# Moving a third exponential tile per batch to VectorE, the combine weights' transposes to another step, and buffers into the order of their release

## The chip, the cores and the metric

One core of a Trainium2 chip. The metric is device time in microseconds, the median of several runs. Ratios are the mean time of one kernel's fast runs over that of the other's of the same rounds, so not quite the ratio of the medians quoted beside them. Ratios use fast runs alone; a median quoted as "measured" is of all runs, and where one of them counts as slow (over 1.5 % above the fastest of its kernel), that is said. The clock is the share of PE's full clock that the profile shows as granted. Engines: PE is TensorE, ACT ScalarE, DVE VectorE, POOL GpSimd, SP SyncE.

## The reference

Attention with a soft cap, then a soft mixture of experts over its output:

```python
# q, k, v: (8 batches, 12 heads, 448, 64), cap 30
scores = cap * tanh((q @ k.T / 8) / cap)
attn = exp(scores - max) / sum                    # x = attn @ v, 3584 x 768
logits = x @ phi                                  # 32 slots, 4 for each of 8 experts
slot_in = softmax(logits, over tokens).T @ x
slot_out[e] = relu(slot_in[e] @ w1[e]) @ w2[e]    # 768 -> 1024 -> 768
out = softmax(logits, over slots) @ slot_out
```

## The kernel before

The attention runs as 56 chunks of six 128 x 448 score tiles, seven chunks a batch. I call them place 0 to 6 of a batch. ACT makes two tanh and one exponential a chunk. PE makes scores ("sc"), attention times V ("pv"), transposes and small sums; most of the latter share one bank of PSUM (`psT`, `bufs=1`), so each waits for the copy of the one before (in the trace before kps waits 0.25 us for zacc, lps 0.48 us for the copy of eps). Of these, kps, qps and xps are transposes of k, q and x, lps the logits, eps the transposed weights of the mixture, and zps and wps their sums over tokens and over slots; zacc and winv are what DVE makes of the two sums. From chunk 8 on, DVE computes the exponential of the first tile in places 1 and 3 as a polynomial:

```python
shared = [j for j in range(NCH - 2) if j % 7 in (1, 3) and j > 7] if cap < 80 else []

def poly_exp(j, part):
    t, bits = exs[j][:, 0, :], 2.0 ** 23
    if part == 0:      # three tensor_scalar operations: exponent and mantissa bits
        ...
    elif part == 1:    # two SBUF inputs from here on
        dve.scalar_tensor_tensor(xp, xm, POW2[1], xm, ALU.add, ALU.mult)
        dve.scalar_tensor_tensor(xp, xp, POW2[2], xm, ALU.add, ALU.mult)
    else:
        dve.scalar_tensor_tensor(xp, xp, POW2[3], xm, ALU.add, ALU.mult)
        dve.scalar_tensor_tensor(t, xp, POW2[4], xe.bitcast(F32), ALU.add, ALU.mult)

def e_norm(b):         # "zps" on PE, "zacc" on DVE
    ps = psT.tile([P, 1], F32, name="zps", tag="T")
    ...                # four matmuls
    dve.tensor_tensor(zacc, ps, zacc, op=ALU.add)

def e_sums(bb):        # "wps" on PE, "winv" on DVE
    ps = psT.tile([P, NT], F32, name="wps", tag="T")
    ...                # seven matmuls
    dve.reciprocal(winv[:, bb, :], ps)

def vcast(Q):          # two POOL casts of V, float32 to bfloat16
    pool.tensor_copy(t[0:HP, :, :, 0:DH], raw[0:HP])
    pool.tensor_copy(t[HP:P, :, :, DH + 1:VW - 1], raw[HP:P])
    ...
```

A table `at(chunk, slot, function, ...)` fixes the order of every engine's instructions: slot "a" is behind the first pv of a chunk, "b" and "c" around the second, "d" at its end. `spare(n)` issues n matmuls of ones ("junk"), which keep PE busy (ten take 0.75 us). After the attention, 20 tiles of w2 ("w2t") are loaded into the SBUF that its buffers leave, then two layers and the output follow.

The softmax here doesn't subtract the row's maximum and nothing guards it: scores larger than these inputs give would overflow.

## Time and profile before

| | before |
|---|---|
| time, first three runs | 315.85 us (315.2 to 318.35) |
| last pv ends | 267.2 us |
| output starts, span ends | 281.1, 313.9 us |
| ACT, PE, DVE, POOL busy | 89, 87, 61, 44 % |

The row of PE's clock is one digit a fortieth of the span, 9 for full speed:

```profile
PEclk9999999999999999999999999999999999999995
```

### The profile page before, as it was taken

How to read it: one execution, taken by the hardware profiler on the slowest of the kernel's cores; microseconds unless marked ns; L12 is line 12 of the kernel's file. 1: busy time of each engine (PE TensorE's matmuls, PEld its weight loads, DVE VectorE, ACT ScalarE, POOL GpSimd, SP SyncE). 2: the span in 40 equal slices, each digit the busy share in tenths (PEclk: the TensorE clock that was granted, in tenths of full speed). 3: DMA queues.
4: the chain of work that ended last, by engine and by line, in shares of the span. 5: the costliest groups of instructions: out<-in, count | busy, mean ns of one | idle time of the engine just before them, and what ended most of it. 6: DMA issues, size and time to landing. Idle time of an engine off the chain costs nothing.

```text
span 313.9 us, 9348 instructions
## 1 busy us (share of the span) xinstructions
PE 271.9 (87%) x4071; PEld 190.6 (61%) x4071; DVE 191.4 (61%) x479; ACT 278.3 (89%) x208; POOL 137.3 (44%) x178
## 2 busy tenths in 40 slices
PE   8899998989899989898989998989898898998620
PEld 6676666666676666666666666666676578643300
DVE  3624567846785578457855885578557765336740
ACT  4999999999999999999999999999999999226630
POOL 5473662655455554474457426652753020200000
PEclk9999999999999999999999999999999999999995
DMA  7999999899999999999799999999999617799996
GB/s 267 195 211 195 205 195 231 131 183 234 216 153 201 222 210 160 209 186 229 122 191 215 194 186 194 223 214 177 164 212 170 156 51 255 249 406 349 397 413 248
DMA packets 57481, 67.64 MB, mean 215 GB/s; under 512 B 3808, under 2 KB 53600, under 8 KB 57440
## 3 DMA queue, kind: packets, MB, share of 16 engines
q0 software_dynamic: 42448, 35.31, 73.4%
q1 hardware_dynamic: 14704, 31.50, 28.6%
q8 instruction: 32, 0.52, 0.6%
q10 hardware_dynamic: 288, 0.23, 0.3%
q14 instruction: 9, 0.07, 0.1%
HBM read 91.32 MB, written 18.87 MB: 351 GB/s over the span
## 4 chain that ended last, share of the span: by engine, by line
ACT 69%; PE 13%; DMA 7%; DVE 5%; issue 2%; SPq 1%; DVEq 0%; ACTq 0%
ACT ex L286 36%; ACT ex L290 32%; DMA w2t<-w2d 5%; PE pv L326 4%; DMA out_dram<-ob 2%; PE sc L277 2%; PE junk L515 1%; PE boot L515 1%; DVE xq L337 1%; PE op L763 1%; ACT ob L772 1%; PE xps L352 1%; DVE obh L721 1%; PE pvl L326 1%; PE pvm L326 1%
## 5 line engine op out<-in xcount | busy, mean ns | idle before, releaser
L286 ACT ACTIVATE ex<-sc 128x1344 bf16<-128x1344 f32 (+1 forms) x113 | 163.7, 1720 | 0.8 <-PE sc L277 0.8
L290 ACT ACTIVATE ex<-ex 128x2688 bf16<-128x2688 bf16 (+4 forms) x58 | 158.0, 2753 | 0.1
L326 PEld LDWEIGHTS <-ex 128*128 128x128 bf16 x1344 | 78.0, 97 | 23.7 <-DVE xq L337 13.7
L326 PE MATMUL pv<-vbd,ex 128*128 128x130 bf16 x1274 | 89.3, 220 | 2.5 <-DVE xq L337 0.8
L277 PE MATMUL sc<-qT,kT 64*64 64x448 bf16 x672 | 78.6, 358 | 5.2 <-ACT ex L286 4.3
L255 POOL CAST vbd<-vraw 64x896 bf16<-64x896 f32 x23 | 22.2, 963 | 66.9 <-PE pv L326 42.7
L336 DVE RECIPROCAL rec<-pv 128x4 f32<-128x4 f32 x91 | 16.5, 182 | 42.6 <-PE pv L326 42.6
L380 POOL COPY e<-E 128x512 bf16<-128x512 bf16 x9 | 6.7, 746 | 81.3 <-ACT E L374 49.2
L337 DVE TENSOR_TENSOR xq<-pv,rec 128x256 bf16<-128x256 f32 x91 | 38.6, 424 | 3.2
L277 PEld LDWEIGHTS <-kT 64*64 64x64 bf16 x672 | 27.0, 105 | 22.3 <-issue 4.2
L515 PEld LDWEIGHTS <-ones 128*128 128x128 bf16 x428 | 26.0, 101 | 10.6 <-DVE xq L337 6.0
L515 PE MATMUL junk<-ones 128*128 128x128 bf16 x391 | 29.1, 220 | 3.1 <-DVE xq L337 2.6
L247 DVE COPY kT<-kps 128x896 bf16<-128x896 bf16 x23 | 14.3, 623 | 18.1 <-PE kps L245 18.0
L256 POOL CAST vbd<-vraw 64x896 bf16<-64x896 f32 x23 | 23.9, 1041 | 1.3
L109 POOL DMA_DIRECT2D w1b<-in_moe_w_dram x32 | 24.5, 766 | 0.0
L354 DVE COPY xT<-xps 128x512 bf16<-128x512 bf16 x47 | 19.5, 414 | 1.0 <-PE xps L352 1.0
L352 PE MATMUL xps<-ident,xq 128*128 128x128 bf16 x188 | 18.1, 218 | 0.8 <-DVE zacc L391 0.2
L167 POOL DMA_DIRECT2D qb<-in_q_dram x22 | 16.2, 736 | 3.8 <-DMA kraw<-in_k_dram 3.1
L247 DVE COPY qT<-qps 128x896 bf16<-128x896 bf16 x23 | 14.2, 618 | 5.5 <-PE qps L245 5.5
L245 PE MATMUL qps<-ident,qb 128*64 128x128 bf16 x308 | 12.8, 222 | 4.1 <-DVE lg L368 4.0
L167 POOL DMA_DIRECT2D kb<-in_k_dram x22 | 16.0, 728 | 0.0
L113 POOL DMA_DIRECT2D w2d<-in_moe_w_dram x20 | 15.1, 761 | 0.0
(117 smaller groups left out, 280.4 us busy)
## 6 DMA issues: line engine op xcount, KB each, us to landing
w1b<-in_moe_w_dram POOLq DMA_DIRECT2D x32, 384.0 KB, 8.8
vraw<-in_v_dram SPq DMA_DIRECT2D x23, 448.0 KB, 6.3
w2d<-in_moe_w_dram POOLq DMA_DIRECT2D x20, 384.0 KB, 8.9
w2t<-w2d SPq DMA_DIRECT2D x20, 384.0 KB, 5.8
out_dram<-ob SPq DMA_DIRECT2D x8, 768.0 KB, 8.6
qb<-in_q_dram POOLq DMA_DIRECT2D x22, 224.0 KB, 7.2
kb<-in_k_dram POOLq DMA_DIRECT2D x22, 224.0 KB, 8.2
w2b<-in_moe_w_dram POOLq DMA_DIRECT2D x12, 384.0 KB, 8.1
```

Source lines behind the costliest of these rows:

```text
L109: pool.dma_start(out=w1b[e][:, js, fs], in_=w1r[:, e, js, fs])
L167: (sp if nm == "v" else pool).dma_start(out=t, in_=quad_ap(nm, Q))
L247: dve.tensor_copy(t, ps)
L255: pool.tensor_copy(t[0:HP, :, :, 0:DH], raw[0:HP])
L256: pool.tensor_copy(t[HP:P, :, :, DH + 1:VW - 1], raw[HP:P])
L277: pe.matmul(sc[cs, u, 0:S], qkT["k", Q][r, c, cs], qkT["q", Q][r, :, cs], start=True, stop=True)
L286: act.activation(exs[j][:, half * CS + u0:half * CS + u1, :], sc[:, u0:u1, 0:S], ACT.Tanh, scale=qk_scale / cap)
L290: act.activation(exs[j][:, u0:u1, :], exs[j][:, u0:u1, :], ACT.Exp, scale=cap)
L326: pe.matmul(pvs[pr, half][:, n, 0:VW], exs[j][:, u, GOFF[g]:GOFF[g] + P], vbds[Q % 2][:, h, c, :], start=(c == 0 and n == 0), stop=(c == N ...
L337: dve.tensor_tensor(xq[Q][:, 2 * half:2 * half + 2, h * P:(h + 1) * P] .rearrange("p g (i d) -> p g i d", i=2), pv[:, :, :, 0:DH], rec.to_ ...
L352: pe.transpose(ps[:, g, :], xq[Q][:, g, h * P:(h + 1) * P], ident)
L515: pe.matmul(junk if home is None else home, ones, ones, start=True, stop=True)
```

## The change

Its intent: ACT bounds the attention, so take six more tiles from it (places 5); make room on PE and in the transpose bank there by moving the weights' transposes ("eps") and their sums to the next batch's place 1; and lay out SBUF so that the w2t loads find freed buffers early.

```diff
+    hpad = consts.tile([P, E, NFT, NS], BF16, name="hpad")        # was in the tail
+    px = att.enter_context(tc.tile_pool(name="px", bufs=1))       # xe, xm, xp: were last
     qk = att.enter_context(tc.tile_pool(name="qk", bufs=2))
-    vb0, exps (bufs=4), vb1, xs
+    ex0, ex1, vb0, ex2, ex3, vb1 (a pool each), xs
...
-    shared = [... j % 7 in (1, 3) and j > 7]
+    shared = [... j % 7 in (1, 3, 5) and j > 7]
...
-                at(j + 12, "d", e_transp, b)
+                at(j + 15, "c", e_transp, b)
...
-                at(j + 14, "d", e_sums, b // 2)
+                at(j + 15, "d", e_sums, b // 2)
...
-        for slot, part in (("a", 0), ("c", 1)):
-            at(j, slot, poly_exp, j, part)
-        at(j + 1, "b" if j % 7 == 1 else "a", poly_exp, j, 2)
+        for part, (dj, slot) in enumerate(((0, "a"), (0, "c"), (1, "b" if j % 7 == 1 else "a"))
+                                          if j % 7 < 5 else ((0, "c"), (1, "a"), (1, "c"))):
+            at(j + dj, slot, poly_exp, j, part)
...
+    at(3, "d", pool.memset, hpad, 0.0)
```

More of the change, by code (lines that the diff above doesn't have):

```diff
@@ L130 @@
     ldv = att.enter_context(tc.tile_pool(name="ldv", bufs=1))
+    px = att.enter_context(tc.tile_pool(name="px", bufs=1))
+    xe, xm, xp = (px.tile([P, S], dt, name=nm)
+                  for nm, dt in (("xe", I32), ("xm", F32), ("xp", F32)))
     qk = att.enter_context(tc.tile_pool(name="qk", bufs=2))
-    vb = [att.enter_context(tc.tile_pool(name="vb0", bufs=1))]
-    exps = att.enter_context(tc.tile_pool(name="exps", bufs=4))
-    vb.append(att.enter_context(tc.tile_pool(name="vb1", bufs=1)))
+    exps, vb = [], []
+    for nm, home in (("ex0", exps), ("ex1", exps), ("vb0", vb), ("ex2", exps), ("ex3", exps),
+                     ("vb1", vb)):
+        home.append(att.enter_context(tc.tile_pool(name=nm, bufs=1)))
     xs = att.enter_context(tc.tile_pool(name="xs", bufs=4))
-    xe, xm, xp = (xs.tile([P, S], dt, name=nm, tag=nm, bufs=1)
-                  for nm, dt in (("xe", I32), ("xm", F32), ("xp", F32)))
     attp = ExitStack()
@@ L282, in tanh_chunk @@
         if half == 0:
-            exs[j] = exps.tile([P, CH, S], BF16, name="ex", tag="ex")
+            exs[j] = exps[j % 4].tile([P, CH, S], BF16, name="ex", tag="ex")
         sc = scores.pop(i)
@@ L293, in exp_chunk @@
         exp_part(j, 1 if j in shared else 0, CH)
-    shared = [j for j in range(NCH - 2) if j % 7 in (1, 3) and j > 7] if cap < 80 else []
+    shared = [j for j in range(NCH - 2) if j % 7 in (1, 3, 5) and j > 7] if cap < 80 else []
     def poly_exp(j, part):
@@ L632 @@
     tl = ctx.enter_context(tc.tile_pool(name="tl", bufs=1, reuse_waits="tile"))
-    hpad = tl.tile([P, E, NFT, NS], BF16, name="hpad")
-    pool.memset(hpad, 0.0)
     w2t = {}
```

## The prediction

> **What bounds the kernel now.** I read the page first, then the chain of waits in order of time, then the timelines of TensorE (PE), VectorE (DVE) and GpSimd (POOL) over one batch, and last the stretches of the tail. The page's chain, then pieces of the chain in order of time:
>
> ```profile
> ACT 69%; PE 13%; DMA 7%; DVE 5%; issue 2%; SPq 1%; DVEq 0%; ACTq 0%
> ```
> ```profile
> 47.27 2.36 ACT ex L286 x2
> 49.62 1.96 ACT ex L290
> 51.59 2.36 ACT ex L286 x2
> 53.95 2.33 ACT ex L290
> ```
>
> From 6.9 us to 223 us the end hangs on ScalarE (ACT) without a gap: two tanh and one exponential a chunk. A chunk whose first tile VectorE takes over shows 1.96 instead of 2.33: 0.37 us saved. From 223 us on, the same chain runs through PE and DVE with no wait on ACT, 44 us long; pieces of it, with fillers ("junk"), normalisations ("xq") and the polynomial ("xe", "xm") in it:
>
> ```profile
> 238.31 0.33 DVE xT L354
> 238.64 0.31 DVE xe L302
> 238.97 0.41 DVE xm L304
> 239.40 0.39 DVE xe L306
> 239.79 0.10 DVE rec L336
> 239.92 0.43 DVE xq L337
> 240.35 0.05 issue
> 240.40 0.75 PE junk L515 x10
> ```
>
> So the attention is balanced: ACT sets the pace, and PE with DVE in its loop is just behind. How little PE has to spare is in its waits on ACT ("PE sc <- ACT ex": 4.3 us in 12 waits). In the PE timeline they come at 158.91 (0.28), 177.67 (0.12), 191.20 (0.28), 209.97 (0.49) and 223.49 (0.28). Locks at 62.02 and 223.49 are five batches (of seven chunks) apart: 161.47 / 5 = 32.29 us a batch. Left to itself PE would need 32.29 - 0.28 - 0.12 = 31.9 us in an odd batch (one that also forms "wps") and 32.29 - 0.28 - 0.49 = 31.5 in an even one. The scores are double buffered: counted to the end of ACT's preceding instruction (its recorded starts drift early), they are 1.7 us or more ahead of a tanh in most of the steady part.
>
> The tail: at 267 us attention ends. The stretches after it (length, then PE, weight load, DVE, ACT, POOL busy, clock, DMA share, GB/s):
>
> ```profile
> 264.00:272.00 8.00, 7.71 (x148) 6.44 (x145) 3.42 (x13) 3.54 (x7) 2.33 (x2) 1.00 0.77 272
> 272.00:282.00 10.00, 9.74 (x185) 4.70 (x185) 3.68 (x9) 2.77 (x5) 0.02 (x1) 1.00 0.98 382
> 292.00:311.00 19.00, 5.34 (x33) 2.48 (x31) 7.83 (x10) 5.98 (x7) 0.00 (x0) 0.85 1.00 404
> ```
>
> PE is full until about 280; from 281 to 311 the 11 MB of output keep the DMA engines full. In between, PE waits for the last w2t load only 0.34 us.
>
> [...] the polynomial's undisturbed steps show 615 to 625. [...] this carries my prediction (POOL, then DVE):
>
> ```profile
> 206.88 1.04 POOL L255 CAST vbd<-vraw 64x896 bf16<-64x896 f32 x1 [3.07 <-PE pv L326]
> 207.98 1.24 POOL L256 CAST vbd<-vraw 64x896 bf16<-64x896 f32 x1
> ```
> ```profile
> 207.60 0.80 DVE L308 SCALAR_TENSOR_TENSOR xp<-xm 128x448 f32<-128x448 f32 x1
> 208.43 1.26 DVE L309 SCALAR_TENSOR_TENSOR xp<-xp,xm 128x448 f32<-128x448 f32 x1
> ```
>
> Beside the V casts the pair takes 2.09 us instead of 1.2, and the casts take 1.04 and 1.24 instead of 0.93 and 0.95.
>
> **The change part by part.** I call chunks 0 to 6 of a batch by their place.
>
> (1) ACT. Six more first tiles (chunks 12, 19, 26, 33, 40, 47) leave it: 6 x 0.37 = 2.2 us. This is worth something only if PE keeps up: 31.92 us a batch.
>
> (2) DVE gets seven operations each: 0.38 + 0.39 + 0.39, 0.71 + 0.96, 0.62 + 0.63 = 4.1 us, 24.5 us in all, placed after the q copy of place 5 and in place 6. The "eps" transpose and its copy leave place 5. Place 5 to the next batch's place 0 before:
>
> ```profile
> 192.79 0.58 PE L245 MATMUL qps<-ident,qb 128*64 128x128 bf16 x14
> 193.31 0.76 PE L277 MATMUL sc<-qT,kT 64*64 64x448 bf16 x6
> 194.13 0.38 PE L399 MATMUL eps<-ident,e 128*128 128x128 bf16 x4
> 194.99 0.35 PE L363 MATMUL lps<-phib,xT 128*128 128x32 bf16 x8 [0.48 <-DVE ET L400]
> ...
> 199.09 0.58 PE L245 MATMUL kps<-ident,kb 128*64 128x128 bf16 x14 [0.25 <-DVE zacc L391]
> 199.60 0.58 PE L326 MATMUL pv<-vbd,ex 128*128 128x130 bf16 x7
> ```
>
> From qps to the next pv is 6.81 us. Taking out eps brings lps forward by 194.99 - 194.13 = 0.86. But in DVE's queue the first normalisation of place 6 now stands behind the whole new work. Start-to-start times from the trace, from qps: norm begins at 0.11; +0.56 norm, +0.60 q copy, +1.15 part 0, +0.30 logits, +0.56 norm, +0.33 xT, +1.20 part 1, +0.56 norm = 5.4. Part 2 then starts while POOL makes its two V casts, which are released by the pv that ended at about 4.8 (before: 197.97, casts from 198.04). Both of its operations have two SBUF inputs, so I take 2.1 us as at 207.60, not 1.2: 7.5. Then zacc (0.16), which holds the one transpose bank that kps needs: kps at 7.6, pv at 8.1. That is +1.3 us on PE a batch, the 0.86 already used up; without the collision it would be +0.4.
>
> (3) "eps" lands in place 1 behind the second pv, where PE waits 0.30 to 0.38 for a normalisation: about +0.06.
>
> (4) "wps" (odd batches 1, 3, 5) leaves place 0: 171.88 - 171.26 = 0.62 gained. In its new place its reciprocal stands in DVE's queue behind part 1 of place 1's polynomial, which ends at 177.76 before and at about 178.0 with the ET copy ahead of it. Until then the transpose bank is held, so the xps that started at 176.38 starts at about 178.2; 14 fillers follow, and the scores of 177.67 start at about 179.3: +1.6 us, the ACT wait of 0.12 included.
>
> Sum on PE: an even batch 31.5 + 1.3 + 0.06 = 32.9; an odd one 31.9 + 1.3 - 0.62 + 1.7 = 34.3. Both exceed ACT's 31.92, so ACT begins to wait for PE after one or two batches. From the lock at 62 to that at 223: three even, two odd batches, 167.3 against 161.5 = +5.8; then 1.3 - 0.62 + 1.7 = +2.4 up to the end, where no wait on ACT is left to absorb it. Attention ends about 8 us later, nothing of the 2.2 us kept.
>
> (5) Buffers. Before, w2t loads are issued at 244, then 256 (the second lies on vraw and waits for the last V cast), 258, 262, and 13 of 20 only from 267.27 on. With hpad gone from the head and the pools in order of release, I count from tile sizes that about two can go near 246, five by 258, twelve by 265 and three are left near 270 (times as if attention ended as before). They finish before layer 2 needs them. Worth: the 0.34 us wait and what of w2t is still moving when output starts, about 0.2 MB at 400 GB/s, together 0.5 us. The hpad memset (1.8 us on POOL) was hidden and stays so.
>
> Total: 315.85 + 8 - 0.5 = 323; I shade it to 321.5, since the collision of part 2 is inferred from another place (3 to 5 us hang on it).
>
> **The rivals.** (a) PE keeps up, ACT stays the bound: -2.2 - 0.5, 313. For it: DVE is 61% busy, moving eps gives PE 0.86 us just where DVE gets work, and the placement looks deliberate. Against it: place 6 holds 2.3 us of DVE work before and gets 2.9 to 3.8 more in 4.3 us. (b) The DVE burst fits but for the wps stall: six times 0.4 instead of 1.3 takes 5.4 off, 318. (c) Buffers count for more, since DMA is 7% of the chain: 4 us. Against it: output is full from 281 to 311 whatever w2t does, and PE's start of layer 2 waits for no load. (d) PE's clock falls in the new gaps of over 1 us: up to 326; nothing in the trace before shows such a gap in the steady part.
>
> **Range and chances.** My sum has some seven chances in ten, centred on 322 with 2 us to either side; the rest lies between 313 and 318. 8 in 10: 313.5 to 325.5. Faster by over 2% (under 309.5) would need more than ACT and tail can give: 0.03. Slower by over 2% (above 322.2): 0.42. Within: 0.55.
>
> **What would show it.** Right: ACT waits for PE's scores from the third batch on, some 10 us in all; the new part 2 near 1.2 us an operation, beside casts; kps waiting on zacc over 1 us in place 6; xps in odd batches waiting over 1 us for winv; the chain in PE and DVE for most of the span; attention ending near 275. Wrong: ACT without gaps, and its end near 265; then PE found idle time that I didn't see, or POOL's casts came at another moment. The buffers: more w2t loads issued before the last pv, and no w2t in the chain.

One paragraph of the recorded text is cut where it is marked: it quoted figures and a rule from elsewhere, which no trace here shows as they were put. The sum came to 315.85 + 8 - 0.5 = 323 us, shaded to 321.5, and its 0.37 us for a shorter exponential and 2.1 us for part 2 were read from the trace. 615 to 625 is in ns.

What the trace before shows of the collision: the polynomial's first two operations with two SBUF inputs take 0.61 to 0.63 us where no POOL cast or copy runs beside them; beside a V cast the first takes 0.80 to 0.86 us, the second 1.25 to 1.26, in seven places each. DVE's other operations that fall beside casts do not change: `xe<-xe` (one input) stays at 0.39 to 0.40 us, `xq<-pv,rec` (pv in PSUM) at 0.42. Of ACT's recorded starts: the exponential recorded at 237.71 with 3.32 us reaches 0.99 us past the recorded start of the next tanh, 240.04. In rival (d), "over 1 us" is the size of the gaps in this forecast and not a threshold; the trace before has the clock at 0.50 only in the output's drain (from 306 us on), where PE has no work.

## The result

| | before | changed |
|---|---|---|
| median | 317.1 us (315.2 to 318.47, 4 runs) | 331.25 us (330.65 to 331.65, 4 runs) |
| ratio of fast runs | 1 | 1.045 (1.038 to 1.052) |
| last pv ends (profile) | 267.2 | 282.6 |
| output starts, span ends | 281.1, 313.9 | 296.6, 328.9 |
| granted PE clock over the span | 0.986 | 0.950 |

Slower, and outside my range. On the rounds of the experiments below, the kernel before had medians of 315.8 to 315.9 us. The loss lies in the attention (15.4 us later). From the last pv to the end it is 46.2 us instead of 46.7.

The page's chain, which was 69 % ACT, and ACT's group of tanh instructions with its idle time and what ended most of it:

```profile
PE 40%; DVE 33%; ACT 18%; DMA 3%; issue 2%; DVEq 0%; ACTq 0%
...
L291 ACT ACTIVATE ex<-sc 128x1344 bf16<-128x1344 f32 (+1 forms) x113 | 141.3, 1317 | 15.0 <-PE pv L331 7.7
```

ACT now waits 15.0 us before its tanh instructions, for work of PE; 0.8 before. PE and DVE set the end. Place 6, first POOL, then DVE, then PE (start, length, engine, line, operation; in brackets the idle time before and what ended it):

```profile
209.34 0.93 POOL L260 CAST vbd<-vraw 64x896 bf16<-64x896 f32 x1 [2.93 <-PE pv L331]
210.31 1.25 POOL L261 CAST vbd<-vraw 64x896 bf16<-64x896 f32 x1
```
```profile
209.53 0.42 DVE L342 TENSOR_TENSOR xq<-pv,rec 128x256 bf16<-128x256 f32 x1
209.87 0.88 DVE L316 SCALAR_TENSOR_TENSOR xp<-xp,xm 128x448 f32<-128x448 f32 x1
210.78 1.25 DVE L317 SCALAR_TENSOR_TENSOR ex<-xp,xe 128x448 bf16<-128x448 f32 x1
211.96 0.15 DVE L396 TENSOR_TENSOR zacc<-zps,zacc 128x1 f32<-128x1 f32 x1
```
```profile
209.89 0.25 PE L392 MATMUL zps<-ones,e 128*128 128x1 bf16 x4
212.16 0.58 PE L250 MATMUL kps<-ident,kb 128*64 128x128 bf16 x14 [2.02 <-DVE zacc L396]
```

Part 2 runs beside the casts and takes 0.88 and 1.25 us. The ends follow one another: part 2's first operation ends 0.48 us after the first cast, the second cast (1.25 us) 0.81 after that operation, and part 2's second operation 0.47 after the second cast. The tiny zacc stands behind it, and kps waits 2.02 us for zacc's bank. An odd batch's place 1, PE alone (xps waits 1.03 us for winv in two of the three such batches, 0.37 in the third):

```profile
186.72 0.33 PE L414 MATMUL wps<-ones,ET 128*128 128x1 bf16 x7 [0.45 <-DVE ET L405]
186.91 0.72 PE L521 MATMUL junk<-ones 128*128 128x128 bf16 x10
188.65 0.38 PE L357 MATMUL xps<-ident,xq 128*128 128x128 bf16 x4 [1.03 <-DVE winv L415]
```

And what I had not counted, the clock row of the page, and one such place in three stretches of 3.41 us (bounds, length, busy time of PE, PE's weight loads, DVE, ACT, POOL, then the granted clock):

```profile
PEclk9999999987999799979997999999988999999975
```
```profile
241.59:245.00 3.41, 1.40 (x20) 0.87 (x18) 3.30 (x6) 3.41 (x4) 2.77 (x3) 1.00 1.30 204
245.00:248.41 3.41, 3.40 (x38) 2.76 (x37) 1.36 (x4) 2.46 (x2) 1.56 (x3) 0.50 1.21 246
248.41:251.82 3.41, 3.34 (x61) 2.48 (x56) 1.63 (x5) 2.23 (x2) 0.00 (x0) 1.00 1.28 211
```

In the stretch with the wait PE is busy 1.40 of 3.41 us. In the next one its clock is 0.50, although it has work all the time: 38 matmuls where the one after holds 61, and 14 pv take 1.70 us (at 245.90) where the next 14 take 0.98 (at 248.66). The profiled run has five such dips, 20.5 us in all; if half the clock doubled PE's time and all of it counted, that would be at most some 10 us lost (an estimate).

### The profile page after: what moved, and what is told of

It reads as the page before. It is cut to its first block, busy times and chain, and to the rows that moved or that the text cites. A ratio compares the mean times of both kernels' runs of the same rounds, so it can differ in the third digit from the quotient of the medians.

```text
span 328.9 us, 9405 instructions
## 1 busy us (share of the span) xinstructions
PE 279.5 (85%) x4071; PEld 195.9 (60%) x4071; DVE 214.9 (65%) x521; ACT 278.6 (85%) x208; POOL 141.3 (43%) x178
## 4 chain that ended last, share of the span: by engine, by line
PE 40%; DVE 33%; ACT 18%; DMA 3%; issue 2%; DVEq 0%; ACTq 0%
PE pv L331 14%; ACT ex L291 9%; ACT ex L295 8%; PE sc L282 7%; DVE xq L342 6%; DVE xp L314 3%; DVE ex L317 3%; PE junk L521 3%; PE xps L357 3%; PE kps L250 3%; DVE xp L316 2%; DVE xp L313 2%; DVE xm L309 2%; DVE rec L341 2%; DMA out_dram<-ob 2%; DVE xe L311 2%
## 5 line engine op out<-in xcount | busy, mean ns | idle before, releaser
L291 ACT ACTIVATE ex<-sc 128x1344 bf16<-128x1344 f32 (+1 forms) x113 | 141.3, 1317 | 15.0 <-PE pv L331 7.7
L295 ACT ACTIVATE ex<-ex 128x2688 bf16<-128x2688 bf16 (+4 forms) x58 | 132.1, 2282 | 0.1
L331 PEld LDWEIGHTS <-ex 128*128 128x128 bf16 x1344 | 81.7, 100 | 24.5 <-DVE xq L342 11.4
L331 PE MATMUL pv<-vbd,ex 128*128 128x130 bf16 x1274 | 93.2, 226 | 2.3 <-DVE xq L342 0.8
L282 PE MATMUL sc<-qT,kT 64*64 64x448 bf16 x672 | 80.1, 367 | 1.7 <-ACT ex L291 1.5
L260 POOL CAST vbd<-vraw 64x896 bf16<-64x896 f32 x23 | 23.1, 1006 | 69.5 <-PE pv L331 50.6
L261 POOL CAST vbd<-vraw 64x896 bf16<-64x896 f32 x23 | 26.4, 1149 | 1.2
L250 PE MATMUL kps<-ident,kb 128*64 128x128 bf16 x308 | 14.2, 236 | 12.2 <-DVE zacc L396 9.8
L250 PEld LDWEIGHTS <-kb 128*64 128x64 bf16 x308 | 11.3, 118 | 17.8 <-issue 17.7
L357 PEld LDWEIGHTS <-xq 128*128 128x128 bf16 x188 | 14.1, 102 | 7.7 <-issue 7.7
L314 DVE SCALAR_TENSOR_TENSOR xp<-xp,xm 128x448 f32<-128x448 f32 x20 | 17.8, 890 | 0.7
```

The source lines that it names most:

```text
L250: pe.transpose(ps[h * HP:h * HP + HP, c, :], src[:, h, c * DH:(c + 1) * DH], ident)
L282: pe.matmul(sc[cs, u, 0:S], qkT["k", Q][r, c, cs], qkT["q", Q][r, :, cs], start=True, stop=True)
L291: act.activation(exs[j][:, half * CS + u0:half * CS + u1, :], sc[:, u0:u1, 0:S], ACT.Tanh, scale=qk_scale / cap)
L295: act.activation(exs[j][:, u0:u1, :], exs[j][:, u0:u1, :], ACT.Exp, scale=cap)
L331: pe.matmul(pvs[pr, half][:, n, 0:VW], exs[j][:, u, GOFF[g]:GOFF[g] + P], vbds[Q % 2][:, h, c, :], start=(c == 0 and n == 0), stop=(c == N ...
L357: pe.transpose(ps[:, g, :], xq[Q][:, g, h * P:(h + 1) * P], ident)
```

## The experiments

Theories. **Queue and clock**: DVE's queue makes PE wait in place 6 (because of the collision with the casts) and in odd places 1 (because of where the sums stand), and those waits also halve PE's clock for a while. **Queue alone**: the clock costs little. **Layout**: the new buffers cost the time. **Weights**: moving the transposes does. Twelve kernels ran, all correct except one. Where the changed kernel is compared below, its time is 331.25 us. The three runs that count as slow (in `e3_fill`, `e4_no_cast`, `e5_early`) are the ones with their kernel's lowest clock, so leaving them out of the ratios hides part of the clock's effect there.

### One part at a time

`e1_buffers`: `j % 7 in (1, 3)`, and e_transp and e_sums at their old places; only the buffers stay changed.

> The buffers in the order of release (with hpad among the constants) and nothing else. If DVE's queue and PE's clock make the loss, this is a kernel as fast as before: ratio 0.995 to 1.002, the w2t loads in the chain no more, clock 0.98 to 0.99. If the new layout makes the loss (its addresses, or the early memset), ratio 1.03 or more and the clock falls as in the changed kernel.

Measured 315.11 us against 315.76, ratio 0.998 (0.997 to 1.000), clock 0.98. The layout costs nothing and gives about half a microsecond. As worked out, two w2t loads were issued at 246.7 and 247.3, five more by 258.9; before, the second waited until 256.

`e2_no_third`: everything but the third tile.

```diff
-    ... j % 7 in (1, 3, 5) and j > 7
+    ... j % 7 in (1, 3) and j > 7
```

> The whole change without the third exponential tile (buffers and the moved transposes and sums stay). If the third tile's DVE work makes the loss: ratio 0.995 to 1.01, since the 1.7 us that the reciprocal of the sums costs PE in odd batches fits into the lead of 2.7 us that the scores have there; ACT without gaps over 0.3 us until its last batch. If the move of the transposes makes the loss: ratio 1.02 or more.

Measured 316.58 us, ratio 1.005 (1.000 to 1.011), and no wait of ACT in the attention among its longest. Layout and weights alone are not the cause; the loss needs the third tile.

### The clock

`e3_fill`: fillers where PE waits in place 6.

```diff
                 at(j + 13, "d", e_norm, b)
+                at(j + 13, "d", spare, 24)
```

> The changed kernel with 24 filler matmuls on PE in place 6, between zps and kps, where PE waits for zacc anyway. If half of the loss is PE's halved clock after that wait: no stretch at half clock in the attention, clock back to 0.98 or more, 5 to 7 us faster than the changed kernel, 323 to 326 us, which is what my sum without the clock gave. If the queue alone makes the loss and the clock costs little: within 1 us of the changed kernel, as kps still starts when zacc is done.

Measured 326.32 us (326.08 without the slow run), ratio 1.032 (1.029 to 1.035): 5 us back by adding work. But one stretch of 10.2 us at half clock stayed in the profile. It began at 181.79, at the end of an odd batch's wait for winv of 1.02 us. Of its runs the fastest (325.14 us) had the clock at 0.981, the slowest, counted as slow, 334.41 us at 0.941. So the expectation of no stretch at half clock failed, for a reason the next one tests.

`e9_fill_both`: the same, and 18 more fillers in the odd batches' place 1.

```diff
                 at(j + 15, "d", e_sums, b // 2)
+                at(j + 15, "d", spare, 18)
```

> The changed kernel with fillers in both long waits: 24 in place 6 before kps, and 18 in the odd batches' place 1 before xps, where PE waits for the sums' reciprocal. In the fill of place 6 alone one run still had a stretch at half clock that began at the odd batch's wait. If those waits are what halves the clock: no stretch at half clock before the end in any run, all runs within 1 us of each other at 324.5 to 326 us; what is then left over the kernel before, 9 to 10 us, is DVE's queue alone. If the clock falls for another reason: half-clock stretches stay.

Measured 323.36 us, ratio 1.023 (1.017 to 1.029), clock 0.982 to 0.987 in all four runs. In the profile the attention ends at 275.1, and the clock is full until the output drains:

```profile
PEclk9999999999999999999999999999999999999985
```

DVE's queue is as before, part 2 as slow as ever (DVE):

```profile
235.93 0.88 DVE L316 SCALAR_TENSOR_TENSOR xp<-xp,xm 128x448 f32<-128x448 f32 x1
236.84 1.25 DVE L317 SCALAR_TENSOR_TENSOR ex<-xp,xe 128x448 bf16<-128x448 f32 x1
238.02 0.15 DVE L396 TENSOR_TENSOR zacc<-zps,zacc 128x1 f32<-128x1 f32 x1
```

and kps still starts only when zacc is done:

```profile
238.22 0.58 PE L250 MATMUL kps<-ident,kb 128*64 128x128 bf16 x14 [0.63 <-DVE zacc L396]
```

So the clock's share is 331.25 - 323.36 = 7.9 us, and what the change costs at full clock, its gains taken off, 323.36 - 315.92 = 7.4 us. Each is good to about 1.5 us, by the spread of these runs. The time came out 1 us below what I expected, and the runs spread over 3 us instead of 1, without a difference of clock to explain it. The kernel before has such runs too: in the same rounds 318.34 and 318.64 us at a clock of 0.980, beside 315.36 to 315.96. That spread is left open.

### The queue: casts and sums

`e4_no_cast`: the V casts of place 6 left out in the batches with a third tile (a wrong result).

```diff
-        pool.tensor_copy(t[0:HP, ...]) ; pool.tensor_copy(t[HP:P, ...])
+        if Q % NQB or Q < 6:
+            pool.tensor_copy(t[0:HP, ...]) ; pool.tensor_copy(t[HP:P, ...])
```

> The changed kernel without the two GpSimd casts of V in place 6 of batches with a third tile (their V load stays; the result is wrong on purpose). If the casts make part 2 slow: its two operations take 0.62 us each instead of 0.85 and 1.25, kps waits 1.0 to 1.2 us instead of 2.0, PE's clock stays up, and the time is 319 to 322 us. If the collision is of no weight: the wait stays near 2 us and the time within 1 us of the changed kernel. If the collision counts but the clock does not: 325 to 327 us.

Measured 318.92 us (318.3 without a slow run), ratio 1.009 (1.006 to 1.012), about as expected; no half clock in the profile, and kps waits 1.12 us. The slow run, 324.95 us, had its clock at 0.952, so "PE's clock stays up" failed in one run of four. DVE in place 6:

```profile
232.69 0.61 DVE L317 SCALAR_TENSOR_TENSOR xp<-xp,xm 128x448 f32<-128x448 f32 x1
233.34 0.62 DVE L318 SCALAR_TENSOR_TENSOR ex<-xp,xe 128x448 bf16<-128x448 f32 x1
233.88 0.15 DVE L397 TENSOR_TENSOR zacc<-zps,zacc 128x1 f32<-128x1 f32 x1
```

Part 2 takes 1.2 us to the start of zacc instead of 2.1. Two POOL instructions a batch, on an engine that is 43 % busy, decide over 12 us, part of it by way of the clock. Leaving them out also frees POOL for other work; `e7_early_sums` below keeps them and moves part 2 instead.

`e6_sums`: the sums two places later, in place 3.

```diff
-                at(j + 15, "d", e_sums, b // 2)
+                at(j + 17, "b", e_sums, b // 2)
```

> The changed kernel with the sums of the weights (wps and its reciprocal) two places later in place 3, all else as it is. If the reciprocal behind part 1 costs what I predicted (1.6 us in three odd batches): 3.5 to 5.5 us faster than the changed kernel, 326 to 328 us, and no wait of xps over 0.4 us. If the scores' lead hides it: within 1.5 us of the changed kernel.

Measured 326.78 us, ratio 1.035 (1.032 to 1.039). Six stretches at half clock remain, 20.5 us in all, each beginning at the end of place 6's wait of 2.0 to 2.2 us or within 1.1 us after it.

`e12_sums_fill`: that and the 24 fillers of place 6, so both at full clock.

> The changed kernel with the sums of the weights in place 3 and 24 fillers in place 6. It takes the odd batches' wait away besides the clock. If the sums' reciprocal costs 1.6 us in each of three odd batches: 4 to 5.5 us faster than with the fillers in both waits, 319.5 to 321.5 us, and no half clock. If it is hidden: 324 us or more.

Measured 318.78 us, ratio 1.010 (1.005 to 1.015), below the range expected by 0.7. Against the fillers in both waits: 323.36 - 318.78 = 4.6 us, the cost of the sums' place at full clock (with the little that the 18 fillers add). Against `e6_sums`, which differs by the 24 fillers alone: 326.78 - 318.78 = 8.0 us, the clock's price a second time. What is left of the third tile in its place, over the kernel without it (`e10_no_third_sums`, below, in the same rounds): 318.78 - 315.27 = 3.5 us.

`e8_old_weights`: buffers and third tile, transposes and sums where they were.

> Buffers and third tile as in the changed kernel, but the weights' transposes and sums at their places before the change. If the moved transpose gave PE its 0.86 us where DVE's queue decides anyway (as I worked out, used up), and the moved sums cost 1.6 us three times: between 4 us faster and 3 us slower than the changed kernel, 327 to 334 us. If the moved transposes are what pays for the third tile: 336 us or more.

Measured 330.07 us, ratio 1.046 (1.042 to 1.051). Its profiled run (329.93 us) has only two short half-clock stretches (6.8 us), which can cost 3.4 us at most; at full clock it would be at 326.5 us or more (an estimate), above the 323.36 us of the moved weights. So moving the transposes does help PE, and what the sums lose is less; no run shows it at full clock. In it kps waits 2.0 to 2.2 us in place 6, and before that lps 1.1 to 1.3 us in place 5. A wait of 2 us is then not always followed by half the clock. The changed kernel shows this too: its kps at 212.16 waits 2.02 us, and no dip follows. What decides is open (last section).

### Versions that keep the third tile

`e5_early`: its three parts half a place earlier, so that part 2 is over before the casts start.

```diff
-  ... if j % 7 < 5 else ((0, "c"), (1, "a"), (1, "c"))
+  ... if j % 7 < 5 else ((0, "a"), (0, "c"), (1, "a"))
```

> The changed kernel with the third tile's three parts half a place earlier (part 0 behind the first pv of place 5, part 1 behind its q copy, part 2 behind the first pv of place 6), so that part 2 is over before the casts begin. All else as in the changed kernel. If what costs is where part 2 stands: its operations take 0.62 us, kps waits under 0.3 us for zacc, no stretch at half clock; the reciprocal behind part 1 in odd batches still costs 1.7 us three times, partly in the lead of the scores: 313.5 to 317 us. If DVE simply has too much work in places 5 and 6: 322 us or more.

Measured 320.25 us (319.3 without a slow run at a clock of 0.959), ratio 1.010 (1.005 to 1.015): between the two outcomes. kps waits 0.25 us, as foreseen, but one stretch at half clock is left (6.8 us), and the runs follow the clock: 316.90 us at 0.980, 319.30 at 0.970, 321.20 at 0.964. Two odd batches still wait 1.02 us for winv, the last at 177.4. The stretch is not there: it begins at 230.09, behind a wait that the new place makes, of lps for q's copy, which now stands behind part 0:

```profile
227.93 0.35 PE L368 MATMUL lps<-phib,xT 128*128 128x32 bf16 x8 [1.21 <-DVE qT L252]
```

`e7_early_sums`: that and the sums in place 3.

> Both moves together: the third tile half a place earlier and the sums in place 3. If both theories hold, PE needs under 31.5 us a batch, ACT is the bound again and its six shorter exponentials come through: 2.2 us and the buffers' 0.5 us under the kernel before, 312.5 to 314 us, ACT without gaps over 0.3 us. If something else in the change holds PE up: 315.5 us or more.

Measured 313.32 us (313.06 to 313.98, 5 runs), ratio 0.992 (0.991 to 0.993), as expected: faster than both kernels. Place 6 in it, POOL and then DVE:

```profile
229.78 0.93 POOL L260 CAST vbd<-vraw 64x896 bf16<-64x896 f32 x1 [4.04 <-PE pv L331]
```
```profile
228.50 0.61 DVE L316 SCALAR_TENSOR_TENSOR xp<-xp,xm 128x448 f32<-128x448 f32 x1
229.15 0.62 DVE L317 SCALAR_TENSOR_TENSOR ex<-xp,xe 128x448 bf16<-128x448 f32 x1
229.75 0.18 DVE L341 RECIPROCAL rec<-pv 128x4 f32<-128x4 f32 x1
```

On PE, kps waits 0.25 us again, as before the change:

```profile
230.84 0.58 PE L250 MATMUL kps<-ident,kb 128*64 128x128 bf16 x14 [0.25 <-DVE zacc L396]
```

Part 2 is over when the casts begin, and the kernel has the same instructions as the changed one: 331.25 against 313.32 us by order alone. It keeps the wait of lps in place 5 (0.85 to 1.21 us in three batches), but the clock is 0.978 to 0.980 in all five runs.

`e10_no_third_sums`: the same without the third tile.

> The fast version (third tile half a place earlier, sums in place 3) without its third tile. If the six shorter exponentials make its gain: 315 to 315.5 us, 2 us slower than it. If the gain comes from the weights' places or the buffers: 313.5 us or less.

Measured 315.27 us, ratio 0.998 (0.994 to 1.002). So the third tile itself gains 315.27 - 313.32 = 1.95 us when placed well, of the 2.2 us that six shorter exponentials are.

`e11_old_buffers`: `e7_early_sums` with the buffers of the kernel before.

> The fast version with the buffers of the kernel before (hpad in the tail, pools in the old order). If the order of release is worth the 0.5 us that it showed alone: 313.6 to 314.2 us. If a shorter attention makes the w2t loads the bound without it: 315 us or more.

Measured 313.55 us, ratio 0.991 (0.988 to 0.995). The order of release is worth 0.2 us here, within the noise; the shorter attention does not make the loads the bound.

So of the theories "queue and clock" stands. "Queue alone" falls by the fillers, "layout" by `e1_buffers`, and "weights" as the whole cause by `e2_no_third`; the sums' new place costs little without the third tile.

## Why the prediction was right or wrong

- **What bounds the kernel, right.** ACT with PE and DVE just behind. The changed kernel's chain is 73 % PE and DVE. Two readings were a little off, without consequence: the chain before has "issue" pieces of up to 1.03 us between ACT's, and an even batch has a further wait of PE for ACT of 0.09 us.
- **Part 2 beside the casts, right.** I took 2.1 us for the pair from the place where it was seen before; it came out at 0.88 and 1.25. Taking the casts away brought 1.2 (0.61 and 0.62 us, as the undisturbed steps in the trace before).
- **kps behind zacc, right.** pv of the next place 0 would follow qps after 8.1 us by my count; in the profile it is 212.67 - 204.52 = 8.15. Rival (b), no collision, fell; with the casts taken away (`e4_no_cast`) the time is near its 318.
- **The sums, right.** The wait of xps for winv was 1.03 us in two of three odd batches, and the sums' place cost 4.6 us at full clock where I had counted three times 1.6.
- **The sum on the queue, right.** "+8 us" less 0.5 for the buffers, 323 us, attention ending near 275. With the clock kept up it was 323.36 us and 275.1. That it agrees to 0.4 us is luck: those runs spread over 3 us.
- **The clock, wrong, and this is the step that failed.** I had it as rival (d), "PE's clock falls in the new gaps of over 1 us: up to 326; nothing in the trace before shows such a gap in the steady part", and left it out of sum and range. But my own count held that gap: it has pv end at 4.8 us and kps start at 7.6, and between them PE has only scores and zps, which take it to some 5.7. That leaves 1.9 us in which PE has nothing to do; the profile shows 2.02, and half the clock in five stretches that begin in such a wait or within 1.3 us of its end. The trace before could not show what such a gap does, for it had none. The clock's cost measured 7.9 us (8.0 in the second pair), as much as the queue itself, where I had allowed some 3. So the range ended at 325.5 instead of some 332.
- **Shading to 321.5, wrong in direction.** The collision that I doubted was there in full.
- **ACT "without gaps", rival (a), fell.** It is what the well-placed version does, at 313.32 us; I put that rival at 313. It needs the parts elsewhere.
- **The buffers, right in size.** 0.5 us alone, and rival (c), 4 us, fell. The sum was loose: 0.2 MB at 400 GB/s (404 in the trace from 292 to 311 us) are 0.5 us by themselves, without the wait of 0.34.

## What to carry to other kernels

Before giving an idle engine more work, write out its queue at the spot where the work will stand, and look for a small operation behind it that holds a shared bank: DVE, busy 65 % of the span, stopped PE for 2.02 us here, by way of a zacc of 0.15 us. Try not to place a `scalar_tensor_tensor` with two SBUF inputs beside such POOL casts: here part 2 took 0.88 and 1.25 us with them, 0.61 and 0.62 without (`e4_no_cast`). When a change opens a gap of 1 to 2 us on PE, count its clock as a possible cost of its own (half clock followed waits of 1.02 to 2.2 us here often, not always, and cost 7.9 us in the changed kernel); filling that gap with idle matmuls is a cheap way to measure it.

## What the runs show of the clock and the collision, and what stays open

- In the changed kernel half clock followed 3.41 us stretches in which PE was still busy, 1.40 us of the one from 241.59 to 245.00, around a wait of 2.02 us. The dips last 3.41 or 6.83 us, in `e3_fill` 10.2.
- What decides whether a wait is followed by half the clock, the runs don't settle. In `e6_sums` the stretch at 171.29, 3.41 us long and followed by half clock, has PE busy 1.24 us. In `e8_old_weights`, whose waits in place 6 are 2.0 to 2.2 us, the stretch from 210.20 to 213.61 has PE busy 1.51 us, and full clock follows; in the changed kernel half clock follows the one at 67.50 with 2.25 us, and full clock the one at 210.90 with 2.15 us. So neither the length of the wait nor PE's busy time in such a stretch decides alone. That half clock comes with these waits is shown by the two kernels with all long waits filled or removed (`e9_fill_both` and `e12_sums_fill`, clock 0.977 to 0.987 in all eight runs).
- A scalar_tensor_tensor beside a cast on POOL loses time, and so does the cast: 0.88 and 1.25 us with the casts, 0.61 and 0.62 without, and 1.25 instead of 0.95 for the cast that found the operation under way. Each of the three lost a little less than the overlap, by 0.13 to 0.15 us (the second operation overlaps the second cast by 0.78 us and loses 0.63).
